# A retention and squared-ReLU kernel: the order keys of its planner and its no-operations are dealt out anew

## The chip, the cores and the metric

The kernel runs on one core of one Trainium2 chip. The metric is the device time of one execution in microseconds (us). "The span" is the time from the first to the last instruction in a profiled execution; the device time is a little longer.

## What is computed

Two layers in a row. First, retention (attention with a decay in place of the softmax) for 8 batches, 8 heads, 576 positions and a head dimension of 64; then a feed-forward layer with a squared ReLU on the 4608 rows of 512 that come out.

```python
scores = scale * np.matmul(q, k.transpose(0, 1, 3, 2))
ret = scores * Dmat[None]                 # Dmat = gamma_h ** (i - j) where i >= j, else 0
attn = np.matmul(ret, v)                  # (8, 8, 576, 64)
x = attn.transpose(0, 2, 1, 3).reshape(4608, 512)
h = x @ w_in                              # (4608, 2048)
out = np.maximum(h, 0) ** 2 @ w_out       # (4608, 512)
```

All inputs and outputs are float32; the kernel multiplies in float16.

## The kernel before

**Units, pairs and groups.** A unit is 128 positions of one batch with all heads (or the two 64-position tails of two batches); there are 36. Two units make a group, 18 in all. The first eight units are loaded and transposed in pairs (`add_unit_pair`, `add_ret_pair`); from unit 8 on each unit goes by itself (`add_load`, `add_unit`).

**One unit from 8 on.** SP (SyncE) issues the loads of k, v (L441; for tails L444, two halves) and q (L438, four pieces) into one of five slots. POOL (GpSimd) casts k and q to float16 (L516, L527) and scales v (L532). SP then issues a DMA that transposes k and q into a tile `kqT` (L543), which waits for the two casts. Six such tiles exist.

**One group on TensorE.** The retention part is a run of small 64x64 matmuls (`quad`, L502), four of them side by side in the array. From group 4 on the output part of group g and the scores (`psc`) and state sums (`psS`) of group g+1 stand in one run (`f0` in `add_ret`). VectorE masks the scores (L838), updates the states (L859, L863, L611) and multiplies the outputs into `xT` (L898). The feed-forward part is large matmuls: `ph` (L1229), 16 column blocks with 4 matmuls each of 256 columns; ScalarE takes the ReLU (L1237), ScalarE or VectorE the square (L1247, L1249) into `gT`; then the products `po` (L1327) by one level of Strassen, with sums `gS` of VectorE (L1300), copies of ScalarE (L1340) and adds of VectorE (L1350) into `o`, which SP stores (L1011, tails L1016). For three late groups the first layer goes by Strassen too (L1072).

**What sets the order.** The kernel does not issue its work directly. Every piece of work is a task of the class `Schedule`, with an engine, a planned duration, the tasks it depends on, the buffers it needs, and a key. `emit` goes through a planned time: whenever an engine is free it starts the ready task with the lowest key whose buffers are free. The order in which tasks start there is the order in which the instructions of every engine, and of SP's DMA queue, are then issued. The planned time itself is thrown away; on the chip only the order and the semaphores remain. The keys are not computed: the table `PLACES` holds one number for each of the 1828 tasks (of 10^6 and more for the warm-up matmuls).

**No-operations.** After the order is found, `place_runs` deals out no-operations on TensorE. `PADS` holds one number for each run of more than 190 instructions (there are 13); that many no-operations are spread over the large matmuls of 8 instructions or fewer that stand between the run before and this one (`between`), issued by `sched.filler` after those tasks.

Of the kernel before, what the change touches and what calls it, by code (L numbers as in the profile page):

```python
# [21 lines left out]
1001812 1001813 1001814 1001815 1001816 1001817 1001818 1001819 1001820 1001821 1001822 1001823 1001824 1001825 1001826 1001827 78 79 80 81 82 83 9 84  # L22
10 85 13 86 16 87 18 88 22 89 25 90 26 91 92 93 94 95 96 97 259 260 262 263 265 266 268 269 11 12 14 15 28 29 17 19 21 20 23 24 43 44 45 46 54 55 47
49 51 50 52 53 172 174 175 178 190 191 179 181 184 182 185 187 275 277 278 280 293 294 281 283 286 284 287 289 98 99 100 340 343 344 66 101 102 103
353 357 358 67 104 105 106 394 396 399 68 107 108 109 404 406 409 69 110 111 112 479 481 484 70 113 114 115 487 489 491 71 116 117 118 539 540 541 2
119 120 121 543 544 27 594 1 658 615 566 607 579 606 608 660 678 613 553 552 648 590 605 640 570 7 556 684 628 633 665 698 153 564 656 677 683 686 560
554 569 689 663 681 679 580 548 48 717 682 694 709 609 558 619 703 718 721 670 576 441 627 687 729 598 692 555 8 589 614 688 731 671 507 597 860 676
693 637 623 546 732 542 639 691 586 587 403 204 584 667 638 616 699 649 577 603 673 668 674 581 551 641 655 624 636 610 644 585 583 437 651 625 652
653 538 557 672 659 666 642 702 657 646 618 701 645 575 706 675 697 559 704 710 705 713 545 547 563 735 714 631 700 599 0 622 629 30 32 33 35 36 31 34
37 38 39 40 41 42 56 58 59 62 63 57 60 61 64 65 124 125 128 129 193 196 197 200 201 195 199 202 203 208 209 212 213 296 300 301 305 306 299 303 304  # L30
308 309 323 324 327 328 401 333 337 335 336 408 415 348 354 349 350 351 352 418 499 6 5 3 1734 4 1764 1744 903 1774 1742 1639 1621 1776 1666 1781 1170
1655 1645 1647 1657 1058 1674 1675 1603 1668 1676 1670 1677 886 1582 1772 1581 1579 1786 1752 1770 1110 1724 1727 1602 1706 1685 1721 1601 952 1595
1792 1703 1623 1596 1789 1598 1076 1751 1652 1671 1626 1649 1616 1611 968 1741 1597 1737 1768 1739 1738 1740 1228 1760 1761 1757 1584 1585 1756 1763
1370 1634 1640 1633 1688 1632 1690 1642 1331 1709 1713 1697 1711 1480 1731 1682 550 1749 1775 1699 1673 1783 1696 1788 122 123 126 130 127 131 132 134
133 135 136 138 137 139 140 142 141 143 144 146 145 147 148 151 149 152 154 156 155 157 158 163 159 161 164 165 166 168 170 173 176 180 183 186 188
189 192 194 198 72 243 244 245 246 247 248 249 250 251 252 253 254 255 256 257 258 206 73 205 207 210 214 211 215 216 219 217 220 221 223 222 224 226
228 227 229 230 233 231 234 235 237 236 238 239 241 240 242 167 171 150 160 162 169 177 261 264 267 270 272 271 273 274 276 279 282 285 288 291 290
292 295 297 218 298 302 307 310 312 225 311 313 314 315 317 316 318 319 320 232 74 75 321 322 325 329 326 330 331 338 332 339 341 345 342 346 355 359
356 360 361 365 362 366 367 369 368 370 371 375 372 376 377 381 363 373 374 379 384 378 380 382 383 386 385 387 388 389 390 391 392 393 397 395 398
400 402 334 405 407 410 411 413 347 412 414 416 417 420 419 421 422 423 364 76 77 424 425 426 428 427 429 430 433 431 434 435 438 436 439 442 444 443  # L40
445 446 450 447 451 452 454 453 455 456 460 457 461 462 466 448 458 459 464 469 463 465 467 468 471 470 472 473 474 475 476 477 478 482 480 483 485
486 432 488 490 492 493 495 440 494 496 500 501 503 502 504 505 506 449 595 593 508 509 510 512 511 513 514 516 515 517 519 521 520 522 523 525 524
526 527 531 528 532 535 537 536 947 789 765 1030 805 726 1748 529 1736 1735 1745 1747 530 696 695 518 650 497 498 534 533 772 1005 975 978 774 1003
949 1049 1044 1753 771 820 780 781 835 1681 819 904 902 818 727 905 832 908 801 1765 664 662 842 1004 837 715 917 971 728 776 844 976 784 775 974 1048
785 831 933 1053 841 861 817 909 828 838 825 1147 791 918 1181 1179 823 1665 1750 1653 1648 1773 1664 802 815 1180 811 919 1178 1176 1197 1224 1182
1200 1212 1203 839 1213 1189 1183 1206 1777 1191 1190 1193 1217 778 1779 1222 1173 1195 1223 834 1247 1218 1024 1187 1644 690 680 1230 1194 788 810
1225 1235 906 763 1227 1234 762 830 1207 1192 856 787 1186 1208 826 872 1047 1045 786 846 1215 1216 852 814 1205 1226 845 1661 1780 1694 1643 1718
1646 1184 961 1229 1198 833 1155 1202 1246 1232 1250 1237 1097 1236 816 1008 1114 1040 1032 1719 1103 1031 1120 1107 847 1714 1059 1081 1039 1132 884
1084 1064 1069 1057 1667 720 719 1033 1011 870 829 1035 1090 813 804 1119 1122 803 848 1108 1100 862 807 1054 1074 806 858 1038 1071 822 859 1080 1092
883 911 1067 1066 885 1762 1702 1679 1604 1600 1678 1065 1063 1068 1070 827 1093 1088 1042 950 936 1043 864 1115 782 988 1174 912 925 1635 794 923 930  # L50
795 821 1669 878 876 868 880 752 893 898 900 901 1684 596 647 921 922 722 892 792 927 753 745 931 1006 773 739 928 851 738 744 866 989 740 750 955 849
751 737 879 888 766 736 874 867 764 1580 1672 1658 1654 1778 1787 890 887 863 889 730 897 899 910 854 1029 871 964 1051 768 948 915 798 853 1705 857
913 894 895 741 1769 881 1139 1111 1123 592 1062 1095 1112 1131 1784 582 588 797 799 742 561 865 924 757 565 1144 1113 734 769 920 1094 562 578 1104
877 591 600 1106 855 602 601 1096 1149 620 604 1109 1159 571 1707 1785 1771 1605 1720 1723 1164 1140 1188 1154 574 934 1153 836 1099 996 929 1012 907
567 1017 1027 993 779 1722 1020 980 1022 1013 999 1704 790 824 812 793 1015 938 953 987 759 1583 621 654 1050 997 1135 573 1018 926 959 568 1037 1010
572 1101 1019 1021 1098 1000 1028 777 1001 1002 783 808 1016 1014 940 951 1117 914 954 985 882 1612 1683 1725 1610 1782 1790 979 982 972 956 1171 973
935 960 869 932 981 944 850 891 937 946 770 958 1793 743 746 748 916 1087 1791 754 760 767 761 998 1025 1077 1157 1162 1613 634 643 809 800 1146 1118
994 1023 943 1172 747 984 1148 1137 873 755 1145 1238 1026 756 1055 1175 1078 1133 1007 957 1151 1161 1204 1130 1167 1166 896 1609 1625 1629 1606 1656
1607 1134 1150 1143 1156 1231 1163 1160 1105 1152 1165 1072 983 967 1177 965 991 992 995 1660 1036 962 969 970 941 1608 1124 1128 1127 1129 1158 1125
1243 1102 1239 1767 711 712 1073 1060 1210 986 1082 1041 1075 1268 1079 990 1286 1254 1126 1121 1168 1249 1116 1242 977 1141 1240 1241 1142 1009 1244  # L60
1214 1056 1089 1209 1221 723 1591 1599 1593 1590 1594 1592 1201 1290 1291 1220 942 1264 1275 1269 1280 1274 1276 1281 1289 1086 1278 1282 1251 1287
1588 1261 1344 1296 1295 758 1663 1366 1319 1377 1337 1052 1374 1371 1373 1372 1766 707 708 1211 1219 963 939 1277 1288 1085 1034 1285 1300 875 1083
1260 1341 1091 1138 1339 1375 725 1199 1336 1380 1196 843 1393 1397 840 1169 1385 1422 1136 1689 1759 1717 1686 1695 1586 1364 1387 1386 1389 733 1378
1417 1395 1420 1384 1396 1401 1407 1185 1347 1345 1376 1334 1726 1416 1332 1329 1390 1046 1730 1406 1322 1324 1325 1259 1327 1338 1461 1470 1628 626
635 1589 1755 1754 1758 1394 716 1429 1421 1245 1357 1587 1379 1311 1728 1346 1314 1333 1733 1258 1318 1419 1317 1418 1423 724 1400 1687 1391 1061
1743 1484 1310 1330 1732 1248 1263 1715 1624 1618 1680 1698 1350 1473 1398 1363 1360 1453 1462 1463 1459 1369 1464 1443 1444 1348 1483 1448 1481 1479
1700 1452 1469 1482 1522 1265 1615 1516 1519 1515 1517 1279 1512 1488 1494 1506 1630 749 632 1746 1691 1708 1729 1323 1255 1472 1353 1283 1343 1693
# [11 lines left out]
class Schedule:  # L79
# [27 lines left out]
    def emit(self):  # L107
# [88 lines left out]
        for t in order:  # L196
            t["fn"]()
            for i in range(t["pad"]):
                self.filler()


    PADS = (136, 0, 0, 0, 121, 0, 84, 0, 76, 0, 0, 0, 0)

    def place_runs(self, tasks):

# [1265 lines left out]
```

## Time and profile before

| | us |
|---|---|
| three runs | 289.55, 284.88, 288.27 |
| their median | 288.27 |
| the profiled execution, its time | 286.22 |
| the profiled execution, its span | 284.5 |

The page of the profile gives busy time and its share of the span by engine (PE is TensorE's matmuls, PEld its weight loads), a strip of 40 slices with busy tenths, the granted TensorE clock and the DMA share, the DMA queues (q1 holds what SP issues, q8 the instructions that are fetched), the chain of work that ended last, and the costliest groups of instructions. A wait is idle time of an engine before an instruction, with what ended it. Busy time of the others in the span: VectorE 195.8, ScalarE 190.6, POOL 87.3 us.

### The profile page before, as it was taken

To read this page: it belongs to the slowest core of one execution; us is meant where nothing else is said; L and a number is where in the kernel's file an instruction comes from. 1 tells how busy PE (TensorE), PEld (TensorE's weight loads), DVE (VectorE), ACT (ScalarE), POOL (GpSimd) and SP (SyncE) were. 2 spreads that over 40 slices of the span, in tenths; PEclk is the share of its full clock that TensorE was granted. 3 is DMA by queue.
4 is the path that set the end of the run, shared out by engine and by line. 5 is a ranking of instruction groups with operands and counts; after the bars stand their busy time and mean duration, and the time that the engine had idled before them with its cause. 6 is when DMAs were issued, how large, how long until landed. Compare 5 with 4: busy or idle time off the path is not lost.

```text
span 284.5 us, 10916 instructions
## 1 busy us (share of the span) xinstructions
PE 277.1 (97%) x4490; PEld 237.7 (84%) x4490; DVE 195.8 (69%) x371; ACT 190.6 (67%) x360; POOL 87.3 (31%) x123
## 2 busy tenths in 40 slices
PE   8899999999999999899999999999999999999994
PEld 3578767888888888788888888888988999899883
DVE  4783489756867769635859485866986889765742
ACT  5659884678495848566575767577657486668830
POOL 6550035445334346434342523353243200000000
PEclk9999999999999999999999999999999999999999
DMA  7999998999997989999989969999998902020205
GB/s 204 291 207 205 261 313 233 155 241 167 197 189 165 225 193 177 195 241 198 234 196 215 208 163 198 200 146 249 200 168 215 193 0 78 2 76 1 76 0 150
DMA packets 119152, 50.00 MB, mean 176 GB/s; under 512 B 94784, under 2 KB 113728, under 8 KB 119104
## 3 DMA queue, kind: packets, MB, share of 16 engines
q1 hardware_dynamic: 114560, 44.84, 73.4%
q0 software_dynamic: 4224, 4.19, 8.9%
q8 instruction: 37, 0.61, 0.9%
q10 hardware_dynamic: 320, 0.26, 0.3%
q14 instruction: 11, 0.09, 0.1%
HBM read 36.70 MB, written 9.44 MB: 162 GB/s over the span
## 4 chain that ended last, share of the span: by engine, by line
PE 84%; DMA 11%; SPq 3%; POOL 1%; issue 0%; DVE 0%; POOLq 0%
PE po L1327 36%; PE ph L1229 31%; PE ph L1072 7%; DMA w_out<-in_moe_w_out_dram 6%; PE psO L502 4%; DMA pair<-in_v_dram 2%; PE po L1270 2%; PE psc L502 2%; PE psS L502 2%; DMA kqT<-kq 2%; SPq L460 1%; DMA loads<-in_v_dram 1%; SPq L463 1%; PE psT L584 1%; POOL w_out L478 1%; SPq L543 0%
## 5 line engine op out<-in xcount | busy, mean ns | idle before, releaser
L1229 PE MATMUL ph<-xT,w_in 128*128 128x256 f16 x960 | 117.4, 273 | 0.0
L1229 PEld LDWEIGHTS <-w_in 128*128 128x128 f16 x960 | 93.3, 98 | 11.8
L1237 ACT ACTIVATE rl<-ph 128x512 f16<-128x512 f32 x120 | 70.4, 590 | 42.3 <-PE ph L1229 41.7
L1247 ACT ACTIVATE gT<-rl 128x512 f16<-128x512 f16 x101 | 63.4, 630 | 2.7
L1327 PEld LDWEIGHTS <-gS 128*128 128x128 f16 x544 | 51.6, 98 | 6.1
L1327 PE MATMUL po<-wT,gS 128*128 128x256 f16 x408 | 54.9, 273 | 0.0
L1327 PEld LDWEIGHTS <-gT 128*128 128x128 f16 x408 | 39.5, 98 | 4.8
L1300 DVE TENSOR_TENSOR gS<-gT,gS 128x512 f16<-128x512 f16 (+1 forms) x51 | 32.3, 640 | 9.9 <-ACT gT L1247 9.2
L532 POOL TENSOR_TENSOR v<-loads,vdec_full 128x512 f16<-128x512 f32 x24 | 27.2, 1133 | 36.1 <-DMA loads<-in_v_dram 33.0
L1327 PE MATMUL po<-w_out,gT 128*128 128x256 f16 x272 | 37.6, 273 | 0.0
L1300 DVE TENSOR_TENSOR gS<-gT 128x1024 f16<-128x1024 f16 x34 | 25.7, 760 | 11.8 <-ACT gT L1247 9.0
L516 POOL CAST kq<-loads 128x512 f16<-128x512 f32 x32 | 22.1, 692 | 34.7 <-DMA loads<-in_k_dram 26.9
L1350 DVE TENSOR_TENSOR o<-po,u 128x256 f32<-128x256 f32 x33 | 13.9, 422 | 22.7 <-PE po L1327 14.6
L527 POOL CAST kq<-loads 128x512 f16<-128x512 f32 x24 | 16.8, 700 | 31.0 <-DMA loads<-in_q_dram 31.0
L1340 ACT COPY u<-po 128x256 f32<-128x256 f32 x34 | 12.4, 368 | 16.6 <-PE po L1327 16.4
L898 DVE TENSOR_TENSOR xT<-psO,gam_full 128x512 f16<-128x512 f32 x28 | 18.6, 683 | 5.8 <-PE psO L502 5.7
L1327 PE MATMUL po<-wT,gT 128*128 128x256 f16 x136 | 18.8, 273 | 0.0
L1327 PE MATMUL po<-w_out,gS 128*128 128x256 f16 x136 | 18.6, 273 | 0.0
L838 DVE TENSOR_TENSOR rT<-psc,mask_full 128x512 f16<-128x512 f32 x24 | 15.7, 681 | 0.6 <-PE psc L502 0.6
L1106 DVE CUSTOM_DVE_ANT_0 gT<-ph,loads 128x512 f16<-128x512 f32 x18 | 12.1, 685 | 4.2 <-PE ph L1072 3.5
L611 DVE TENSOR_TENSOR R<-stmp,dec 128x512 f16<-128x512 f32 (+1 forms) x18 | 13.5, 750 | 0.4
L1350 DVE TENSOR_TENSOR o<-po,p 128x256 f32<-128x256 f32 x18 | 7.6, 422 | 7.2 <-issue 3.5
(101 smaller groups left out, 310.3 us busy)
## 6 DMA issues: line engine op xcount, KB each, us to landing
out_dram<-o SPq DMA_DIRECT2D x32, 256.0 KB, 2.8
loads<-in_k_dram SPq DMA_DIRECT2D x24, 256.0 KB, 4.6
loads<-in_q_dram SPq DMA_DIRECT2D x96, 64.0 KB, 3.1
loads<-in_v_dram SPq DMA_DIRECT2D x24, 256.0 KB, 3.8
w_in<-in_moe_w_in_dram POOLq DMA_DIRECT2D x4, 512.0 KB, 8.9
w_out<-in_moe_w_out_dram POOLq DMA_DIRECT2D x4, 512.0 KB, 14.4
pair_c<-in_k_dram SPq DMA_DIRECT2D x2, 512.0 KB
pair_c<-in_q_dram SPq DMA_DIRECT2D x4, 256.0 KB
```

What stands on the lines that cost most here:

```text
L502: t = nc.tensor.matmul(out_, lhsT=lhsT, rhs=rhs, start=start, stop=True, skip_group_check=True, tile_position=(64 * row, 64 * col))
L516: op(out=out_.rearrange("p (n b a d) -> p n b a d", n=2, b=2, a=2), in_=in_.rearrange("p (a n b) d -> p n b a d", n=2, a=2))
L527: nc.gpsimd.tensor_copy(out=tile_of["kq", u][:, 1].rearrange("p (t a d) -> p a t d", t=4, a=2), in_=tile_of["q32", u].rearrange("p (a t) d ...
L532: nc.gpsimd.tensor_tensor(out=t, in0=tile_of["v32", u], in1=vdec[kind].rearrange("p (h o) -> p h o", o=1).to_broadcast([P, H, D]), op=ALU. ...
L898: nc.vector.tensor_tensor(out=tile_of["x", g].rearrange("p n (s e i) -> p e (n s) i", s=n, e=2)[:, c], in0=y.rearrange("p (o t r) -> p o r ...
L1072: nc.tensor.matmul(out_[:, e], lhsT=left[:, m, fi * P:(fi + 1) * P], rhs=right()[:, m], start=fresh and e == 0 and m == 0, stop=m == HK - ...
L1229: nc.tensor.matmul(tile_of["ph", g, fb][:, j, :], lhsT=w_in16[:, m, fi * P:(fi + 1) * P], rhs=tile_of["x", g][:, m, :], start=(m == 0), st ...
L1237: nc.scalar.activation(out=t, in_=tile_of["ph", g, fb], func=ACTF.Relu)
L1247: nc.scalar.activation(out=t, in_=rl, func=ACTF.Square)
L1300: (nc.gpsimd if eng == "POOL" else nc.vector).tensor_tensor(out=tile_of["S", g][:, k, sl], in0=in0(sl), in1=in1(sl), op=op)
L1327: nc.tensor.matmul(tile_of["pb", g, bank], lhsT=left(i), rhs=right[:, i, :], start=(start and i == 0), stop=(i == HF - 1), skip_group_chec ...
L1350: nc.vector.tensor_tensor(out=o_tile(u)[:, half * HM:(half + 1) * HM], in0=bank(x), in1=tile_of[name, g], op=ALU.add)
```

## The change

Two constants change and nothing else: the numbers of `PLACES` and those of `PADS`. No task, buffer, duration or dependency is touched.

```diff
 PLACES = """
-1001794 1001795 ... 1001827 78 79 80 81 82 83 9 84
-10 85 13 86 16 87 18 88 22 89 25 90 26 91 92 93 94 95 96 97 259 260 262 263 265 266 268 269 11 12 14 15 28 29 17 19 21 20 23 24 43 44 45 46 54 55 47
...
+1001812 1001813 ... 1001827 88 89 90 91 92 93 27
+94 28 95 31 96 34 97 36 98 40 99 43 100 45 101 102 103 104 105 106 299 224 225 226 227 228 229 230 231 29 30 32 33 46 47 35 37 39 38 41 42 65 66 67 68
...
 """.split()
...
-    PADS = (136, 0, 0, 0, 121, 0, 84, 0, 76, 0, 0, 0, 0)
+    PADS = (135, 30, 49, 9, 69, 36, 45, 0, 15, 0, 0, 0, 0)
```

(The first lines of each table are shortened here; all numbers behind the warm-up's are new.)

What it does to the orders, counted in the two built programs: the first 722 rows of TensorE's order (equal instructions that follow each other are one row), 53 of VectorE's, 44 of ScalarE's, 28 of POOL's and 13 of SP's are the same in both; behind them all five differ. The number of instructions of each kind is the same, except for no-operations on TensorE (430 before, 401 after) and semaphore waits. POOL keeps the order of its casts and only waits for other things.

The runs of small matmuls from unit 8 on, numbered 0 to 14 (run 0 has only the scores and sums of group 4; run n, from 1 to 13, has the outputs of group n+3 and the scores of group n+4; run 14 the last outputs). Each reads two transposes. "Matmuls ahead" counts L1229 and L1327, of 256 columns each, in TensorE's order; the last two columns count what SP has issued ahead of the later of the two transposes since the loads of unit 8 began: k or v loads / q loads / half loads of tails / stores.

| run | matmuls ahead, before | after | ahead of the transpose, before | after |
|---|---|---|---|---|
| 0 | 264 | 282 | 5 / 2 / 0 / 2 | 7 / 3 / 0 / 1 |
| 1 | 360 | 368 | 9 / 4 / 0 / 4 | 8 / 4 / 0 / 3 |
| 2 | 468 | 488 | 12 / 6 / 0 / 5 | 13 / 7 / 0 / 4 |
| 3 | 608 | 616 | 16 / 8 / 2 / 6 | 16 / 8 / 8 / 6 |
| 4 | 712 | 688 | 19 / 10 / 12 / 8 | 17 / 8 / 12 / 8 |
| 5 | 856 | 832 | 21 / 11 / 12 / 10 | 21 / 11 / 12 / 10 |
| 10 | 1392 | 1408 | 42 / 21 / 12 / 17 | 44 / 22 / 12 / 17 |
| 12 | 1560 | 1570 | 48 / 24 / 14 / 20 | 48 / 24 / 16 / 20 |
| 13 | 1618 | 1624 | 48 / 24 / 24 / 22 | 48 / 24 / 24 / 22 |

## The prediction

> **What bounds the kernel now.** I read the page first (spans, engines, DMA queues), then the waits of TensorE behind the unchanged start, the chain of work around the one wait found, the DMA queue of that stretch, and last the busy time of the runs of small matmuls (L502).
>
> ```profile
> span 284.5 us, 10916 instructions
> ...
> PE 277.1 (97%) x4490; PEld 237.7 (84%) x4490; DVE 195.8 (69%) x371; ACT 190.6 (67%) x360; POOL 87.3 (31%) x123
> ...
> PEclk9999999999999999999999999999999999999999
> ...
> q8 instruction: 37, 0.61, 0.9%
> ```
>
> TensorE is the bound: 277.1 of 284.5 us, at the full granted clock. A busy PE need not be at its peak, so I looked at the step from one matmul to the next: in the chain, 28 matmuls of L1229 from 63.02 us take 3.06 us, 109 ns each, and L1327 steps at 109 ns too. The waits of TensorE from 41 us on are one line:
>
> ```profile
> engine line waited for: us in total, times, longest us
> PE psc L502 <- DMA kqT<-kq: 1.1, 1, 1.1
> ```
>
> In 240 us TensorE waits once, for a DMA; no late ScalarE or VectorE result shows. The chain of work shows where:
>
> ```profile
> 108.26 4.05 DMA loads<-in_v_dram
> 112.31 4.35 DMA kqT<-kq
> 116.67 0.04 issue
> 116.71 0.32 PE psc L502 x16
> ```
>
> This transpose was issued at 112.31 and landed at 116.67; the scores that read it had begun at 115.30, and their second half starts 1.3 us late. The DMA queues of 41 to 223 us, and the time from a transpose's issue to its landing, say why margins are thin:
>
> ```profile
> DMA packets 102768, 36.34 MB, mean 200 GB/s; under 512 B 92540, under 2 KB 99617, under 8 KB 102734
> ...
> q1 hardware_dynamic: 102734, 35.85, 98.3%
> ```
>
> ```profile
> DMA to landing us min/median/max: 3.1/4.5/5.3
> ```
>
> The 16 DMA engines are full (98.3%). TensorE is the bound and DMA stands close behind it: what counts is how early each transpose (L543) lies in SP's queue against the place of its scores in TensorE's. The runs of small matmuls, each with the same 128 matmuls, differ too (columns: window, length, PE busy, weight loads, clock, DMA share, GB/s):
>
> ```profile
> 132.70:134.70 2.00, 1.29 (x128) 1.18 (x128) 1.00 0.76 214
> 160.40:162.40 2.00, 1.42 (x128) 1.31 (x128) 1.00 1.08 215
> ...
> 207.40:209.40 2.00, 1.49 (x128) 1.34 (x128) 1.00 0.92 205
> 219.40:221.50 2.10, 1.52 (x128) 1.37 (x128) 1.00 0.89 201
> ```
>
> **The change, part by part.**
>
> *Work.* No engine gains or loses work: 4490 matmuls on TensorE, 224 copies and 28 transposes on SP stay. At 109 ns a step that sum cannot move; only waits and the length of the runs can.
>
> *Transposes against scores* (runs 0 to 14 as numbered in the section on the change). Margin = start of the scores less landing of the later of their two transposes (its issue plus the measured, or else the median, landing). Shift = matmuls newly ahead of the run, at 0.109 us, less transfers newly ahead of the transpose. Transfers are priced by the trace's packet records of 41 to 223 us (a 256-byte packet 23.4 ns, 1 KB 65 ns, 2 KB 99 ns, on 16 engines): k or v load or transpose 1.5 us, q load 1.04, half load (L444) 0.75, store 0.8.
> - Run 0: 52.66 + 4.5 = 57.2 against 61.3, margin 4.1; 18 matmuls later (+2.0), two k or v loads and a q load more, a store less (-3.2): 2.9.
> - Run 1: 66.94 + 4.5 = 71.4 against 72.6, 1.2; +0.9 and +2.3: 4.4.
> - Run 2: 79.01 + 4.5 = 83.5 against 85.9, 2.4; +2.2 and -1.8: 2.8.
> - Run 3: 93.44 + 4.5 = 97.9 against 102.5, 4.5; 8 matmuls later (+0.9), six half loads more (-4.5): 0.9.
> - Run 4: 116.67 against 115.35, -1.3; 24 matmuls earlier (-2.6), two k or v and two q loads fewer (+5.1): 1.2.
> - Runs 5 to 13, less the 1.3 us that TensorE is then ahead: 3.0 (run 10: 6.7 + 1.7 - 4.1 - 1.3) or more.
>
> The order takes time from where it was plenty and gives it to runs 1 and 4: least margin -1.3 before, 0.9 after. The wait goes: **-1.3 us**. Late next is run 3, then run 4. Ends: nothing gained (a landing 1.4 us over the median plus an error in the prices uses up run 3's margin and as much again) and 1.3 gained.
>
> *ScalarE and VectorE.* I counted TensorE's work between each matmul and the later one that waits for what another engine makes of it. Least before, without a wait: 9 matmuls (0.98 us) around a copy of L1340 (368 ns), 15 (1.64 us) around a relu of L1237 (590 ns). After: 8 once, and 11 once (1.20 us; a relu behind a square of 630 ns makes 1.22). That costs 0 to 0.11 and 0 to 0.44; no gain, as none of these places waited before. I take 0.1, near the lower ends, because the shortfalls (0.11 and 0.02) are small. In the tail the last matmul of L1229 has 12.0 us of products behind it instead of 10.9, so nothing there is wanted sooner, and both end with three products of 8 matmuls, an add and a store: 0.
>
> *Runs joined and split.* Between 41 and 60 us two runs of small matmuls are joined and one is split, so the count stays. Entering and leaving a run costs 94 + 144 ns over the normal step (at 41.8 and 42.4 us): 0, ends -0.24 and +0.24.
>
> *No-operations.* 430 become 401, at other places. In 122.0 to 132.9 us, ahead of run 5 with 122 of them, TensorE is busy 10.9 of 10.9 us at 109 ns a step: matmuls hide them. What they move is where a run starts in the instruction stream. Against the best of their kind the eight runs of 128 matmuls hold 0.9 us and the three of 112 hold 0.2; all at the best gains 1.1, all at the worst (0.23 x 8 + 0.12 x 3 = 2.2) loses 1.1. The runs at 132.7 and 160.4 start at the same place of a 256-instruction block (69) and took 1.29 and 1.42, so the place alone doesn't set it: 0, both ends kept. The Trainium skill's page "Runtime: NRT & Kernel Launch" (Instruction fetch mechanics) has instructions come in 16 KiB blocks of 256, the next fetched while one executes, the crossing mostly hidden. q8's 37 packets in 0.61 MB agree on the block; by the page the no-operations are worth about 0 and the sum is the same, by the rows -1.1 to +1.1.
>
> *Sum against the profiled execution.* It took 286.22 us for a span of 284.5, so 1.7 lies around the span. 286.22 - 1.3 + 0.1 = 285.0 us, span 283.3. That execution is 2.05 below the median of 288.27. The fastest run, 284.88, is what the profiled one would be without its wait (284.9); the other two hold 3.4 and 4.7 us that the profile does not show. I take them for later landings at the same place: wait = 1.3 + lateness, lateness 2.1 and 3.4. With 0.9 of margin the four executions would wait 0, 0, 1.2 and 2.5, median 0.6. **285.0 + 0.6 = 285.6 us.**
>
> **The rivals.**
> - *The scatter stays.* What parts 284.88 from 289.55 is not lateness of transposes, or it strikes runs 3 and 4 as it struck run 4. For it: DMA at 98.3% hands a delay on to everything behind it, and two margins are about 1 us. Against: the one wait seen is of this kind and its size meets the fastest run. Time: 288.27 - 1.3 = 287.0, up to 285.0 + 3.4 = 288.4.
> - *The runs get shorter.* Their places matter and are dealt well: 285.0 - 1.1 = 283.9. Against: equal places took unequal times.
> - *Run 3 waits in earnest* (the other side). Unit 15's transpose stands behind six more half loads and lands 0.9 us before its scores; each us later than that is a us of TensorE. The kernel is slower than before from a wait of 3.3 us (288.27), and by over 2% (294.0) from one of 9.0, a landing 9.9 us late, 14.4 after issue. For it: SP stands up to 3.2 us before a transpose that waits for POOL's casts, and a w_out load took 14.4 to land. Against: no transpose took over 5.3. Time: 294. The Trainium skill's "TensorE: Matmul & The Clock Gate" (Part 1) says that an idle window of some 3.4 us halves the clock; no run here shows it, the clock being full around the 1.1 us wait; by it (an estimate) this case would cost up to 1.7 us more.
>
> **How the numbers follow.** Forecast 285.6 (0.52); the scatter stays, 287.0 to 288.4 (0.34); shorter runs, 283.9 (0.08); run 3 badly late, 294 (0.04); below 282.5, for which all waits and run losses together (284.88 - 1.1 = 283.8) do not suffice (0.02). The range goes from 283.8 to 288.4 and leaves out the last two and parts of the others. Faster by over 2% is below 282.5: 0.02; slower is above 294.0: 0.04; within: 0.94. 2% is about what a measurement of this kernel can tell from no change; the gain forecast, 0.9%, lies inside it.
>
> **What would show it.** Right: no wait for kqT at run 4, span 283 to 284, runs of after closer together than 4.7 us. Wrong: a wait of psc for kqT at run 3 (about 103 us); waits for ScalarE at L1327 or L1229; runs of 128 matmuls all at 1.29 or all at 1.5; runs of after as far apart as before's.

## The result, and the profile after

| | before | after |
|---|---|---|
| median of 22 executions, us | 285.04 | 287.39 |
| fastest, slowest | 284.12, 289.55 | 286.10, 292.08 |
| ratio after / before, 95% interval | | 1.0076 [1.0052, 1.0099] |
| profiled execution: time, span | 286.22, 284.5 | 287.45, 285.7 |

The changed kernel is 0.8% slower, far inside 2% but clear of zero; the forecast was a gain. The ratios leave out the slowest executions, among them two of the changed kernel's 22 here (291.53 and 292.08 us), and further down four of twelve of the new order with the old no-operations (289.75 to 291.25), two of twelve with the moved ones (291.45, 292.24) and one of twelve of the last kernel (288.45). The median of before over 22 executions is 285.04: the three shown ahead of the prediction (median 288.27) were a poor sample.

The page of after, its first lines:

```profile
span 285.7 us, 10886 instructions
...
PE 277.2 (97%) x4490; PEld 237.4 (83%) x4490; DVE 194.0 (68%) x371; ACT 190.7 (67%) x360; POOL 86.8 (30%) x123
...
PEclk9999999999999999999999999999999999999999
...
q8 instruction: 36, 0.59, 0.9%
```

The work is the same (277.2 us of TensorE, 277.1 before) at the full clock. The waits of TensorE behind 41 us (engine, tile, line, waited for: total, times, longest; `psO` is what the retention outputs are summed in):

```profile
PE psO L502 <- issue: 1.8, 1, 1.8
PE ph L1229 <- issue: 0.3, 1, 0.3
```

The wait for kqT is gone, as forecast. In its place stand two of a kind that before did not have: "issue", time in which TensorE waited for nothing that the profile shows. The chain of work puts them in order of time (start, us, what):

```profile
108.57 0.33 PE ph L1229 x3
108.90 0.33 issue
109.22 4.21 PE ph L1229 x37
...
113.94 0.41 PE psO L502 x40
114.35 1.85 issue
116.20 0.26 PE psO L502 x8
```

The second stop is in the middle of a run of small matmuls (run 4), between two of the same kind, 8 from the run's end. A semaphore is not a likely cause there. I counted TensorE's instructions: with 61 instructions ahead of the kernel's own (the offset at which the stops of all profiles fall on boundaries), both stops lie on a boundary between two blocks of 256 instructions, at the entry of blocks 14 and 15. Measured as the step from one matmul to the next, less the normal step, they are 0.49 and 2.02 us. The packet records of the instruction queue (q8, 16 KiB each) show the rest:

| | block 14 | block 15 |
|---|---|---|
| TensorE enters the block before it | 103.90 | 109.22 |
| the packet of this block starts | 106.12 | 113.87 |
| the packet ends | 107.71 | 114.95 |
| the first matmul of this block starts | 109.22 | 116.20 |

In before no block behind 41 us is entered less than 2.0 us behind the end of its packet; here it is 1.52 and 1.25. The work between the boundaries is what the change altered: big matmuls take about 109 ns for two instructions, small ones about 10, so a block with a run in it is short. From entry to entry, stops and the wait for kqT taken off, blocks 12 to 15 last 5.7, 9.7, 4.1 and 9.5 us before; after, 8.8, 4.8, 5.0 and 10.5. Two short ones now stand in a row, as runs 3 and 4 are 72 large matmuls apart instead of 104 (616 and 688 ahead, 608 and 712 before) and the no-operations are dealt out anew.

The transposes, from issue to landing, 41 to 223 us, and the four runs that stood in the prediction (columns as there):

```profile
DMA to landing us min/median/max: 3.2/4.5/7.1
```

```profile
132.10:134.10 2.00, 1.42 (x128) 1.28 (x128) 1.00 1.08 230
161.50:163.50 2.00, 1.29 (x128) 1.18 (x128) 1.00 1.08 216
211.60:213.60 2.00, 1.45 (x128) 1.30 (x128) 1.00 1.06 206
222.20:224.30 2.10, 1.31 (x128) 1.20 (x128) 1.00 0.83 191
```

One transpose took 7.1 us (issued at 104.12) and cost nothing: its scores began at 113.5. The four runs take 5.47 us in all, 5.71 before.

### The profile page after: what moved, and what is told of

Read it like the earlier page. It is cut to its first block, busy times and chain, and to the rows that moved or that the text cites. A ratio compares the mean times of both kernels' runs of the same rounds, so it can differ in the third digit from the quotient of the medians.

```text
span 285.7 us, 10886 instructions
## 1 busy us (share of the span) xinstructions
PE 277.2 (97%) x4490; PEld 237.4 (83%) x4490; DVE 194.0 (68%) x371; ACT 190.7 (67%) x360; POOL 86.8 (30%) x123
## 4 chain that ended last, share of the span: by engine, by line
PE 93%; issue 3%; POOL 2%; DVE 0%; POOLq 0%; DVEq 0%
PE ph L1229 37%; PE po L1327 37%; PE ph L1072 7%; PE psO L502 5%; PE po L1270 2%; PE psc L502 2%; PE psS L502 2%; PE warm L411 1%; PE psT L584 1%; POOL mask L351 1%; POOL vx L562 0%; POOL w_in L478 0%; DVE o L1350 0%; POOL mask_full L343 0%; POOL mask_tail L343 0%
## 5 line engine op out<-in xcount | busy, mean ns | idle before, releaser
L1229 PE MATMUL ph<-xT,w_in 128*128 128x256 f16 x960 | 116.1, 273 | 0.3 <-issue 0.3
L1229 PEld LDWEIGHTS <-w_in 128*128 128x128 f16 x960 | 93.4, 98 | 12.4 <-issue 0.6
L1327 PEld LDWEIGHTS <-gS 128*128 128x128 f16 x544 | 52.1, 98 | 6.2
L1327 PE MATMUL po<-wT,gS 128*128 128x256 f16 x408 | 55.5, 273 | 0.0
L1327 PEld LDWEIGHTS <-gT 128*128 128x128 f16 x408 | 38.9, 98 | 4.9
L532 POOL TENSOR_TENSOR v<-loads,vdec_full 128x512 f16<-128x512 f32 x24 | 26.4, 1100 | 45.1 <-DMA loads<-in_v_dram 45.0
L1327 PE MATMUL po<-w_out,gT 128*128 128x256 f16 x272 | 37.8, 273 | 0.0
L1300 DVE TENSOR_TENSOR gS<-gT,gS 128x512 f16<-128x512 f16 (+1 forms) x51 | 30.6, 604 | 10.0 <-ACT gT L1247 9.1
L516 POOL CAST kq<-loads 128x512 f16<-128x512 f32 x32 | 21.9, 687 | 30.3 <-DMA loads<-in_k_dram 23.8
L527 POOL CAST kq<-loads 128x512 f16<-128x512 f32 x24 | 16.2, 673 | 28.5 <-DMA loads<-in_q_dram 28.4
L1327 PE MATMUL po<-wT,gT 128*128 128x256 f16 x136 | 19.1, 273 | 0.0
L1327 PE MATMUL po<-w_out,gS 128*128 128x256 f16 x136 | 18.1, 273 | 0.0
L1340 ACT COPY p<-po 128x256 f32<-128x256 f32 x17 | 6.3, 372 | 16.9 <-PE po L1327 16.8
```

What stands on the lines that cost most here:

```text
L516: op(out=out_.rearrange("p (n b a d) -> p n b a d", n=2, b=2, a=2), in_=in_.rearrange("p (a n b) d -> p n b a d", n=2, a=2))
L532: nc.gpsimd.tensor_tensor(out=t, in0=tile_of["v32", u], in1=vdec[kind].rearrange("p (h o) -> p h o", o=1).to_broadcast([P, H, D]), op=ALU. ...
L1229: nc.tensor.matmul(tile_of["ph", g, fb][:, j, :], lhsT=w_in16[:, m, fi * P:(fi + 1) * P], rhs=tile_of["x", g][:, m, :], start=(m == 0), st ...
L1300: (nc.gpsimd if eng == "POOL" else nc.vector).tensor_tensor(out=tile_of["S", g][:, k, sl], in0=in0(sl), in1=in1(sl), op=op)
L1327: nc.tensor.matmul(tile_of["pb", g, bank], lhsT=left(i), rhs=right[:, i, :], start=(start and i == 0), stop=(i == HF - 1), skip_group_chec ...
L1340: nc.scalar.copy(out=t, in_=bank(x))
```

## The experiments

"Theory 1" is late instructions, "theory 2" the order itself (late data), "theory 3" the no-operations by themselves. Ratios stand against the kernel before on the same chip (its median there: 285.01 us for the first four kernels, 285.20 for the moved no-operations and the quarter stores, 284.72 for the last two); "stops" are the excess steps at block boundaries in the profiled execution.

**The new order with the old no-operations.**

```diff
-    PADS = (135, 30, 49, 9, 69, 36, 45, 0, 15, 0, 0, 0, 0)
+    PADS = (136, 0, 0, 0, 121, 0, 84, 0, 76, 0, 0, 0, 0)
```

> The new order with the old no-operations (136, 0, 0, 0, 121, 0, 84, 0, 76). In the changed kernel TensorE stood still for 0.49 and 2.04 us exactly where it went into its 14th and 15th block of 256 instructions; two short blocks (4.77 and 4.96 us of work) lie in a row there. Here the 13th block has 8.4 us of work and the 14th 3.8, and the 15th is wanted some 3 us later. Theory 1, instructions fetched late: no stall at either place, at most 0.5 us at one of the new short blocks (3.1 to 3.8 us of work); 284.9 to 285.6 us against 285.04 before and 287.39 after. Theory 2, the new order of the DMAs and engines makes data late in the executions without a profile: 287.4, the no-operations mean nothing. Theory 3, the new no-operations by themselves: about 285.

Measured: 286.43 us, 1.0042 [1.0025, 1.0059]. No stop at blocks 14 and 15; three of 0.30, 0.30 and 0.34 us at blocks 6, 21 and 29. The stop at block 15 needs order and no-operations together, but the rest of the loss did not go: between theories 1 and 2.

**The old order with the new no-operations** (the same line, the other way round).

> The old order with the new no-operations (135, 30, 49, 9, 69, 36, 45, 0, 15). No two short blocks of 256 instructions stand in a row; the shortest is the 26th with 2.9 us of work, the next 5.1. Theory 1, instructions fetched late: no stall in the stretch around 110 us; behind the 26th block 0 to 1.5 us, as a packet of instructions takes about 1.2 us, is usable about 1.25 us behind its end, and starts up to 2 us behind the entering of the block; 285.0 to 286.5. Theory 2, the order: 285.0. Theory 3, the new no-operations by themselves: 287.4.

Measured: 286.08 us, 1.0050 [1.0026, 1.0073]. Stops of 0.52 and 0.20 us at blocks 25 and 27, none near 110 us, no wait for data. The no-operations alone cost the old order 1 us, by the same kind of stop; theory 2 (285.0) fails here.

**The new order without no-operations behind the first long run.**

```diff
-    PADS = (135, 30, 49, 9, 69, 36, 45, 0, 15, 0, 0, 0, 0)
+    PADS = (135, 0, 0, 0, 0, 0, 0, 0, 0, 0, 0, 0, 0)
```

> The new order, with the 135 no-operations ahead of the first long run kept and the other 266 taken out. Blocks of 256 instructions: the 13th has 8.5 us of work, the 14th 4.9, the 16th only 3.2. Theory 1, instructions fetched late: no stall at the 14th and the 15th block, 0 to 1.5 us behind the 16th; 284.9 to 286.4. Theory 2, the order: 287.4. Theory 3, the no-operations by themselves: 285 or below, with no stall anywhere.

Measured: 286.32 us, 1.0056 [1.0030, 1.0081]. None at blocks 14 and 15, and 1.64 us at block 17, right behind the short 16th, as theory 1 had it. It stands between two large matmuls, in the waits of TensorE:

```profile
PE po L1327 <- issue: 1.5, 1, 1.5
```

**The old order without no-operations behind the first long run** (136 and twelve zeros).

> The old order, with the 136 no-operations ahead of the first long run kept and the other 281 taken out. Now a block of 256 instructions (the 16th) holds almost only a run of small matmuls, 1.83 us of work; the 18th has 3.0 and the 25th 3.1. Theory 1, instructions fetched late: a stall of 0.9 to 2.9 us where the 17th block is entered, which shows as issue time of TensorE with no wait, and up to 1 us behind each of the other two: 286.0 to 289. Theory 2, the order: 285.0, no stall. Theory 3, the no-operations by themselves: 285.0 or below.

Measured: 284.93 us, 1.0000 [0.9981, 1.0019]; no stop. Theory 1 as I sized it missed: the 16th block held only 1.8 us of work, yet the packet of the 17th had started 1.0 us before TensorE entered the 16th and ended 1.5 us before it was wanted. The sequencer runs ahead of the matmuls: behind large matmuls a packet starts up to 2.3 us before the entry, from the tenth matmul of a run of small ones on always 0.7 us or more behind it. So the length of a block alone does not decide; when its packet starts does.

**The new order, no-operations moved,** so that block 15 is wanted later, with blocks 19 on as in the changed kernel.

```diff
-    PADS = (135, 30, 49, 9, 69, 36, 45, 0, 15, 0, 0, 0, 0)
+    PADS = (135, 0, 0, 0, 120, 72, 46, 0, 15, 0, 0, 0, 0)
```

> The new order with no-operations (135, 0, 0, 0, 120, 72, 46, 0, 15): as many ahead of the ninth long run as in the changed kernel, so all blocks of 256 instructions from the 19th on are the same as there; only those of 74 to 147 us are cut elsewhere. The 13th has 8.4 us of work, the 14th 3.9, the 15th 9.7, the 16th 4.0. In all profiles so far TensorE stood still at a block only where it wanted the block less than 1.55 us behind the end of its packet of instructions (8 places), and never where it came 1.8 us or more behind it. Theory 1, instructions fetched late: no stall at blocks 14 and 15, in all 0 to 0.5 us; 284.7 to 285.5 us, 2 us less than the changed kernel. Theory 2, something in the order besides costs time: 286.4, as the two other kernels with the new order.

Measured: 287.31 us, 1.0071 [1.0038, 1.0103]: no gain, though the profile (292.24 us, the slowest execution) has no stop at any block behind 41 us. Theory 1 alone fails. Its waits of TensorE behind 41 us:

```profile
PE po L1327 <- DVE o L1350: 3.3, 1, 3.3
PE psc L502 <- DMA kqT<-kq: 1.6, 1, 1.6
```

Both are at 199 to 207 us: data is late there. This execution stands 4.9 us above the median, so it shows where the slowest ones lose time; it need not show what the median loses.

**The changed kernel and the kernel before with quarter stores.**

```diff
-        kind, b, c = units[u]
+        (kind, b, c), hi = units[u], lo + (hi - lo) // 4
```

> The changed kernel, of whose results each store writes only the first quarter of its columns; the rest of the output is left out. All instructions of TensorE stay. Theory 1 with its reason, that the packet of instructions waits behind the data in the DMA engines: packets start sooner (in the changed kernel up to 4.6 us behind the entering of a block), the stalls of 0.5 and 2.0 us at blocks 14 and 15 go, 284.5 to 285.3 us. Rival: the lateness is TensorE's own (how far ahead it asks), the DMA engines' load means nothing: both stalls stay, 286.9 to 287.4.

> The kernel before with the same quarter stores (three quarters of the output left out): what less DMA traffic gives where no instruction is late. Theory 1: 284.5 to 285.0, 0 to 0.5 us below the kernel before. Rival: the scatter of the kernel before (284.15 to 286.09) is data that lands late, so that it gains about 0.5 us and its runs close up.

Measured: 286.93 us, 1.0054 [1.0027, 1.0081], and 284.82, 0.9995 [0.9970, 1.0021]. Fewer bytes stored help neither. The stop at block 15 stays (2.30 us; its packet starts 3.85 us behind the entry of block 14); that at block 14 is gone. The stores are not what holds the packet back; loads and transposes I did not take away. This profile shows what a longer stop brings. The windows behind it (window, length, PE busy, weight loads, VectorE, ScalarE, POOL, clock, DMA share, GB/s):

```profile
116.00:118.00 2.00, 1.75 (x20) 1.42 (x21) 1.45 (x3) 0.42 (x1) 1.60 (x2) 0.83 0.50 143
118.00:120.00 2.00, 2.00 (x11) 1.45 (x10) 0.44 (x1) 1.52 (x4) 0.61 (x1) 0.50 1.03 229
120.00:122.00 2.00, 2.00 (x17) 1.65 (x16) 0.00 (x0) 1.11 (x3) 0.67 (x1) 0.82 0.60 143
122.00:124.00 2.00, 2.00 (x20) 1.80 (x19) 1.28 (x3) 1.06 (x3) 1.65 (x3) 1.00 0.85 165
```

The granted clock falls to 0.50 and comes back 4 us later; PE is "busy" throughout, but does 11 matmuls in 2 us instead of 20. The changed kernel's own profile in 118 to 124 us has 57 matmuls at 1.00, this one 44 at 0.77: 13 x 0.109 = 1.4 us more.

**Further profiles,** without an edit: the changed kernel twice, the one with the moved no-operations, the kernel before.

> The changed kernel once more, unaltered, for a second profiled execution. Theory 1, instructions fetched late: the long stop of TensorE stands again at the entry of block 15 (of 256 instructions), 1.5 to 2.5 us of issue time inside the run of small matmuls near 115 us; 286.1 to 287.7. Theory 2, data late by chance: other places, waits for kqT or for the add into o, no stop at block 15.

> The same, a third profiled execution. A stop of more than 2.3 us lowered the granted clock to 0.77 for 6 us in the kernel with quarter stores; if one occurs here, the time is 288 to 292 and the clock row shows it.

> The new order with the no-operations moved (135, 0, 0, 0, 120, 72, 46, 0, 15), a second profiled execution: the first fell on a rare late transfer (waits of 1.6 us for kqT and 3.3 us for the add into o, 292.2 us), while its fastest executions took 286.1. Theory 1: no stop at blocks 14 and 15; stops of 0.5 to 1.5 us in all at other blocks, wherever a block is wanted less than 1.55 us behind the end of its packet. Theory 2, late transfers are the rule in the new order: waits for kqT or for the add into o again near 195 to 207 us.

> The kernel before once more, a second profiled execution. My prediction took its 1.1 us wait for kqT as typical. If it is not, this execution has no such wait and no stop at a block, and takes 284.2 to 285.6.

Measured: 288.47, 286.77, 286.47 and 285.02 us. Both profiles of the changed kernel stop at block 15 again, for 1.47 us each. The kernel before has no stop and no wait at all, not for kqT either. The moved no-operations have no stop and waits of 0.3 (add into o) and 0.2 us. The first repeat has a second loss, in its waits of TensorE:

```profile
PE po L1327 <- DVE o L1350: 1.5, 1, 1.5
PE psO L502 <- issue: 1.3, 1, 1.3
```

Follow the first of them back, TensorE, then VectorE, then SP (start, us, engine, line, [idle before <- releaser]):

```profile
204.76 0.82 PE L1327 MATMUL po<-wT,gT 128*128 128x256 f16 x6 [1.54 <-DVE o L1350]
```

```profile
200.08 0.42 DVE L1350 TENSOR_TENSOR o<-po,p 128x256 f32<-128x256 f32 x1 [1.18 <-PE po L1327]
204.28 0.42 DVE L1350 TENSOR_TENSOR o<-po,u 128x256 f32<-128x256 f32 x1 [3.77 <-DMA out_dram<-o]
```

```profile
195.77 0.43 SPq L441 DMA_DIRECT2D loads<-in_v_dram  x1
196.31 4.90 SPq L543 DMA_TRANSPOSE kqT<-kq  x3
201.31 0.52 SPq L1011 DMA_DIRECT2D out_dram<-o  x1
```

TensorE waits for an add of VectorE that frees a result buffer (`po`); the add writes into a buffer whose old contents are still being stored; the store was issued at 201.31, behind three transposes in a row, though its last piece of o was ready at 190.4. In the old order no three transposes stand in a row there.

**That store ahead of the three transposes,** with the changed kernel's no-operations, then with the moved ones.

```diff
-        self.place_runs([t for t in order if t["eng"] == "PE"])
+        order.remove(self.tasks[1289]); order.insert(order.index(self.tasks[271]), self.tasks[1289]); self.place_runs([t for t in order if t["eng"] == "PE"])
```

(The second kernel has the PADS line of the moved no-operations as well.)

> The changed kernel, with one store of o (ready at 190.4 us in the profile, issued at 201.3 behind three transposes in a row on SP) put ahead of the first of the three; the no-operations stay. Two causes are now in view: the stop at the entry of block 15 (1.5 to 2.3 us in all four profiles with these no-operations), and the add into o that waits for this store (0 to 3.3 us of TensorE). If both are real: the stop at block 15 stays, no wait of po for the add into o, the slow end of the executions (288 to 292) is gone; 286.1 to 286.9 as median. If the late store is only a companion of a slow execution: 287.4 and the same spread.

> The same, with the no-operations moved as well (135, 0, 0, 0, 120, 72, 46, 0, 15), so that block 15 is wanted later: both causes undone. If they are what the new order costs: 284.8 to 285.8, level with the kernel before, no stop at block 15 and no wait for the add into o, small stops (0 to 0.5 us) at other blocks. If the new order costs something else: 286.2 or more, as the fastest half of the kernel with the moved no-operations alone took 286.1 to 287.3.

Measured: 286.64 us, 1.0085 [1.0059, 1.0111], and 285.46, 1.0021 [1.0000, 1.0043]. The store alone has the median that was expected, 286.1 to 286.9, but gains nothing against before on that chip (a stop of 1.20 us at block 15 remains in its profile, a wait of 0.2 for the add into o); the moved no-operations alone gained nothing; both together take away most of the loss. 0.2% is left, at the edge of what was measured. The second kernel's profile, an execution of 287.81, holds a wait for one of the transposes that were moved behind, at 199.7 us:

```profile
PE psc L502 <- DMA kqT<-kq: 2.1, 1, 2.1
```

The place at 200 us is thin in more than one way. No version beat the kernel before.

**The balance of the profiles,** against the second profile of before (span 283.2, no stop, no wait):

| profiled execution | span more than 283.2 | stops at blocks | waits of TensorE |
|---|---|---|---|
| changed kernel | 2.5 | 2.51 | 0 |
| changed kernel, repeats | 3.6; 1.7 | 1.47; 1.47 | 1.5; 0 |
| new order, old no-operations | 0.9 | 0.94 | 0.2 |
| old order, new no-operations | 1.4 | 0.72 | 0 |
| old order, no no-operations | -0.4 | 0 | 0 |
| before, first profile | 1.3 | 0 | 1.1 |
| new order, no no-operations | 1.4 | 1.64 | 0 |
| store ahead | 1.6 | 1.20 | 0.2 |
| moved no-operations; repeat | 7.3; 1.5 | 0; 0 | 4.9; 0.5 |
| store ahead, moved no-operations | 2.9 | 0.24 | 2.1 |

Stops and waits make up the difference to within 0.7 us in all but the moved no-operations. Their first profile lacks 2.4, of which the lowered clock behind the wait (0.74, 0.50 and 0.91 in three windows of 2 us from 206 us on) makes 1.7; their repeat lacks 1.0, without a cause found.

## Why the prediction went wrong

- **The no-operations, costed at 0 with ends of -1.1 and +1.1: the step that failed.** It asked where a run *starts* in a block and took the crossing itself as hidden. What counts is whether the next block has come. The five profiles with this order and these no-operations stop at block 15 for 1.20 to 2.30 us, above my upper end; in the changed kernel's own profile the two stops make 2.51 us, where the medians differ by 2.35. The prediction gave the Trainium skill's page "Runtime: NRT & Kernel Launch" (Instruction fetch mechanics): the crossing of a block mostly hidden. That holds for most of the 467 crossings behind 41 us in the fifteen profiles, and fails for 13 of them by 0.2 to 2.3 us; the measurement decides. The order has its part in this too, since it brought runs 3 and 4 nearer to each other.
- **ScalarE and VectorE, 0.1.** I counted TensorE's work between a product and its use, and called the least leads safe. I did not follow what VectorE itself waits for. The add into o hangs on a store in SP's queue: in the changed kernel's profile that store lands at 199.23 + 2.50 = 201.73 and the add starts at 202.39, 0.7 us of margin; in the repeat it came too late and cost 1.5.
- **Transposes against scores, -1.3.** For runs 3 and 4 the mechanism came true: no profile of the new order waits for kqT there, and in the changed kernel's the margins were 2.6 and 2.3 us where I had 0.9 and 1.2. But the gain was not there to be had: of five profiles of the old order only the first has the wait, and before's median of 285.04 is what my forecast called "without its wait" (284.9). The profiled execution was untypical, and I built both terms, -1.3 and +0.6, on a scatter of three executions. Run 10, which I gave a margin of 3.0, waited for 1.6 and 2.1 us in two profiles with moved no-operations. I had priced the later of its transposes 4.1 us later than in before (issued at 187.04); the ten profiles of the new order issue it between 190.02 and 198.26, so 3.0 to 11.2 us later. The five of the old order have it between 184.74 and 187.49. One profile and fixed prices did not show that spread.
- **Runs of small matmuls, 0.** Right in size: all of them behind 41 us, stops and waits taken off, 19.4 and 19.3 us in the two profiles of before, 18.8 to 20.0 in the three of after.
- **The rivals.** "Run 3 waits in earnest" did not come; "the runs get shorter" neither. "The scatter stays" gave the right time (287.0 to 288.4 holds 287.39) for another reason: neither run 3 nor run 4 waited. That my range holds the result is luck.

Shown: the stops are at block boundaries, stand only where a packet ended late, and move with the no-operations; the store is issued late, behind three transposes; and with the store ahead, moving the no-operations brings the ratio from 1.0085 to 1.0021 on one chip. The store's own share is less sure: without and with it, the moved no-operations have the intervals [1.0038, 1.0103] and [1.0000, 1.0043], which overlap a little and come from two chips.

Not shown: why the moved no-operations alone gained nothing. One thought is that the stop made TensorE 2 us late for everything behind it and so hid the lateness of store and transpose near 200 us. That cannot be all. With the old no-operations, in the same new order, TensorE reached run 10 just as early (199.8 us, against 199.4 to 200.1 in the three profiles with moved no-operations) and no transfer was late: the transpose was issued at 190.09 and landed at 194.63. In those three it was issued at 194.80, 197.50 and 198.26. So the transposes themselves came 5 to 8 us later there, and what sets their pace is open. These are the rows of SP in the changed kernel's profile and in the first with moved no-operations; the first of the three transposes is run 10's:

```profile
193.07 6.06 SPq L543 DMA_TRANSPOSE kqT<-kq  x3
```

```profile
197.50 4.25 SPq L543 DMA_TRANSPOSE kqT<-kq  x3
```

Open too: why the packet of block 15 starts 3.7 to 4.6 us behind the entry of block 14 in all five profiles. Ahead of it, from 107 to 109 us, the DMA engines nearly stood still with a transpose under way (104 to 116 us in 40 slices, first the busy tenths, then GB/s):

```profile
DMA  9677699999980000079847728997389999999843
GB/s 232 137 162 171 148 233 261 325 236 145 48 3 5 10 10 18 18 152 314 209 130 123 164 61 222 338 321 191 88 184 251 235 319 271 312 323 341 258 151 86
```

But they moved data again from 109.4 us on, 4 us before the packet started, and in the first profile of before they moved only 6 to 9 GB/s at 179.3 to 180.2, 190.1 to 191.3 and 211.4 to 212.6 us, with no stop behind that.

## What to carry to other kernels

Where an engine takes 256 instructions in a few microseconds, its instruction stream is a transfer like any other: give each block a lead (packet start, some 1.1 us of packet, some 1.2 to 1.5 until use) and look where two dense stretches come close together. A stop of "issue" between two equal matmuls is the sign; count instructions there before looking for a semaphore. And a margin read from one profile is no better than that profile: compare the issue times of several executions before calling it safe, since here one transpose was issued up to 7.5 us apart in eight profiles of the same order of transfers.

## What the runs showed of the hardware

- A block of instructions could be used 1.2 to 1.5 us behind the end of its packet. All 13 stops of 0.2 us or more stand where the block was wanted 1.54 us or less behind that end; five others in that range had none, nor had any of the 449 crossings from 1.6 us up.
- The clock fell after a short stop: to 0.50 after 2.12 us of issue time (quarter stores), costing 1.4 us, and again after a wait of 3.3 us (moved no-operations: 0.58 in 207 to 211 us); not after 1.85 us (the changed kernel), nor after a wait of 2.1 (the last kernel). The Trainium skill's page "TensorE: Matmul & The Clock Gate" (Part 1) gives an idle window of about 3.4 us; here less was enough once.
